# A planner that fences GpSimd's instructions behind VectorE's, and counts slack from TensorE's present lag

## The chip, the cores and the metric

The kernel runs on one core of one Trainium2 chip. Five engines with an instruction queue each work side by side: TensorE (PE; its weight loads are listed as PEld), VectorE (DVE), ScalarE (ACT), GpSimd (POOL) and SyncE (SP), which issues the transfers between HBM and on-chip memory. The metric is the time of one execution on the device in microseconds (us).

## The reference

Three layers, the output of one being the input of the next; inputs are float32.

```python
# attention: q, k, v are (4, 8, 576, 64)
scores = scale * np.matmul(q, k.transpose(0, 1, 3, 2))
mask = (rel >= 0) & (rel < 128)                       # rel = query position - key position
scores = np.where(mask, scores - slope[head] * abs(rel), -1e9)
x = softmax(scores) @ v                               # -> (2304, 512)

# mixture: w_gate (512, 8), w1 (8, 512, 1024), w2 (8, 1024, 512)
P = np.exp(x @ w_gate - max)
for _ in range(8):
    P /= P.sum(1, keepdims=True) + 1e-09
    P /= P.sum(0, keepdims=True) + 1e-09
    P *= N / E
x = sum(P[:, e:e + 1] * (np.maximum(x @ w1[e], 0.0) @ w2[e]) for e in range(8))

# last layer: w_in (512, 2048), w_out (2048, 512)
h = x @ w_in
out = np.maximum(0.01 * h, h) @ w_out
```

## The kernel before

The 2304 tokens form 18 tiles of 128, in five groups `p` of up to two tile pairs (`PAIRS`). Attention goes tile by tile: scores (L570), exponentials, transposed probabilities (L651), values (L669). The two feed-forward layers are cut into 20 chunks of 512 hidden columns, 16 of the mixture and 4 of the last layer. Each chunk is multiplied by a scheme of seven block products (`PRODUCTS`), whose operands are sums and differences of blocks; every float32 operand is a pair of float16 numbers, a high part that ScalarE rounds (L803) and a low part that GpSimd subtracts (L804). The first product of a chunk is L1089 (banks `s`, `sq`), the second L1205 (banks `t`).

Around TensorE the work is shared like this. ScalarE copies `s` to `q` (L1101, L1113) and rounds `h` (L1136, L1142, L1158). VectorE combines bank and copy (`sq`, L1105), makes the sums `s` and some low parts `h` (L1117; L1108 in attention), and adds `t` to the output `acc` (L1218). GpSimd makes the low part of the four sums (`h`, L1161, one for each half of a unit, 180 in all), adds `part` to `acc` (L1216), makes the block sums of the weights (`raw`, `t2`, L964) and their low parts (`w`). For two of seven products, ScalarE's `part` (L1215) and GpSimd's L1216 take the place of L1218. Each chunk's weights are scaled by a power of two, through a diagonal `dg` that VectorE makes (L780).

Between 234 and 1108 us of the trace, beside the mixture's chunks, the last layer's weights, which arrive as 64-bit words, are turned into float32 in 32 pieces, up to three a chunk: VectorE's L1018 takes the exponent, ScalarE's L1021 scales it, VectorE's L1024 adds the sign and L1029 takes the mantissa, ScalarE's L1030 and L1036 convert, GpSimd's L1038 and L1042 put the number together, SP stores it.

The order on every engine is made by a planner (`Plan`) while the kernel is built. All instructions are recorded first. `weigh` gives each a cost; VectorE's instructions that read and write on-chip memory alone, without a PSUM bank, are marked `shared`, since they use a port to that memory together with GpSimd. `deadlines` works back from TensorE's products, laid end to end, to the latest time at which each instruction may end (`latest`). `order` then plays the program through: at each step it takes the engine that can start first, among its ready instructions the one with the earliest `latest`, and tries some swaps. `fix` nails the result down as a fixed order on every engine. Between engines, an instruction waits only for the data and the buffers that it needs.

Of the kernel before, what the change touches and what calls it, by code (L numbers as in the profile page):

```python
# [30 lines left out]
class Plan:  # L31
# [13 lines left out]
    LANDING = 2000.0  # L45
    PER_NS = 350.0
    NEAR = 60.0

    def __init__(self, nc, tc, slots, before, after):
        self.tc = tc  # L50
# [192 lines left out]
    def deadlines(self, products):  # L243


        nodes = self.nodes
        n = len(nodes)
        ends, t, mode = {}, 0.0, "full"
        for i in products:
            t += nodes[i]["cost"] + self.TURN.get((mode, nodes[i]["mode"]), 0)  # L250
            mode = nodes[i]["mode"]
            ends[i] = t
        latest = [ends.get(i, t + 5000) for i in range(n)]
        left = [len(self.behind[i]) + len(self.softly[i]) for i in range(n)]
        room = dict.fromkeys(self.START, t + 5000)
        heap = [(-latest[i], -i) for i in range(n) if not left[i]]
        heapq.heapify(heap)
        while heap:
            i = -heapq.heappop(heap)[1]
            a = nodes[i]  # L260
            eng = a["eng"]
            if eng not in ("PE", "SP"):
                latest[i] = min(latest[i], room[eng])
                room[eng] = latest[i] - a["cost"] + self.START[eng]
            for k in a["before"] | a["starts"] | a["soft"]:
                b = nodes[k]
                end = latest[i] - a["cost"] + (b["cost"] if k in a["starts"] else -self.latency(b, a))
                latest[k] = min(latest[k], end)
                left[k] -= (k in a["before"]) or (k in a["starts"])
                left[k] -= k in a["soft"]  # L270
                if not left[k]:
                    heapq.heappush(heap, (-latest[k], -k))
        return latest

    def order(self, latest):
        nodes, behind = self.nodes, self.behind
        n = len(nodes)
        left = [len(node["before"]) + len(node["starts"]) for node in nodes]
        ready, free = [0.0] * n, dict.fromkeys(self.START, 0.0)
# [5 lines left out]
        empty = {tag: [0.0] * bufs for tag, bufs in self.room.items()}  # L285
        using = {name: len(u) for name, u in self.users.items()}
        closed = dict.fromkeys(self.users, 0.0)
        gpsimd, port, mode = (0.0, 0.0), (0.0, 0.0), "full"
        self.starts = [0.0] * n

        def since(i):

# [9 lines left out]
        def takes(i, t):  # L302

            node = nodes[i]
            cost = node["cost"]
            if node["eng"] == "PE":
                cost += self.TURN.get((mode, node["mode"]), 0)
            elif node["shared"] and gpsimd[0] <= t < gpsimd[1]:
                cost = max(cost, gpsimd[1] - t + cost - node["shared"])
            elif node["eng"] == "Pool" and port[0] <= t < port[1]:  # L310
                cost += max(0.0, port[1] - t - 140)
            return cost

        for _ in range(n):
            choices = []
            for e, w in waiting.items():
                when = [(x, i) for x, i in ((since(i), i) for i in w) if x is not None]
                if when:
                    choices.append((max(free[e], min(when)[0]), e, when))
            t, eng, when = min(choices)  # L320
            at = dict((i, x) for x, i in when)
            near = t + (self.NEAR if eng != "PE" else 0)
            pick = min((i for i in at if at[i] <= near), key=lambda i: (latest[i], i))
            start = max(t, at[pick])
            cost = takes(pick, start)
            if eng != "PE" and eng != "SP":

                for i in sorted((i for i in at if i != pick and at[i] < start + cost), key=lambda i: latest[i]):
                    s = max(at[i], t)
                    c = takes(i, s)  # L330
                    if (latest[i] < latest[pick] and max(at[i], start + cost) + nodes[i]["cost"] > latest[i]
                            and s + c + nodes[pick]["cost"] <= latest[pick]):
                        pick, start, cost = i, s, c
                        break
                if nodes[pick]["shared"] and cost > nodes[pick]["cost"] + 100:
                    other = [i for i in at if i != pick and not nodes[i]["shared"] and at[i] <= start + 100
                             and max(t, at[i]) + nodes[i]["cost"] + cost <= max(latest[pick], start + cost + 200)]
                    if other:
                        pick = min(other, key=lambda i: latest[i])
                        start = max(t, at[pick])  # L340
                        cost = takes(pick, start)
            node = nodes[pick]
            end = start + cost
            if eng == "PE":
                mode = node["mode"]
            elif node["shared"]:
                port = (max(start, gpsimd[1]) if gpsimd[0] <= start < gpsimd[1] else start), end
            elif eng == "Pool":
                gpsimd = start, end
            self.starts[pick] = start  # L350
            free[eng] = end - (self.START[eng] if cost > 100 else 0)
            waiting[eng].remove(pick)
            for tag, _ in node["opens"]:
                empty[tag].remove(min(empty[tag]))
            for name in node["uses"]:
                using[name] -= 1
                closed[name] = max(closed[name], end + (self.FROM_PE if eng == "PE" else 60))
                if not using[name] and name in self.tag_of:
                    empty[self.tag_of[name]].append(closed[name])
            orders[eng].append(pick)  # L360
            for k in behind[pick]:
                ready[k] = max(ready[k], start if pick in nodes[k]["starts"] else end + self.latency(node, nodes[k]))
                left[k] -= 1
                if not left[k]:
                    waiting[nodes[k]["eng"]].append(k)
        self.length = end
        return orders

    def fix(self):
        follows = mybir.DependencyInfo(mybir.DependencyClass.NoSync, mybir.DependencyReason.DATA)  # L370
        products = [i for i, node in enumerate(self.nodes) if node["eng"] == "PE"]
        for picks in self.order(self.deadlines(products)).values():
            line = [ins for i in picks for ins in self.nodes[i]["ins"]]
            for a, b in zip(line, line[1:]):
                self.tc.add_manual_dep(b, a.name, follows, reason="order")


@with_exitstack
# [1115 lines left out]
```

## Time and profile before

| | |
|---|---|
| median of 3 runs | 1856.25 us (1854.02 to 1857.41) |
| the profiled execution | 1853.38 us, span of its records 1851.6 us |
| granted TensorE clock in it | 0.996 of full speed |
| busy: TensorE, its weight loads | 1812.1 us (98%), 1603.7 us (87%) |
| busy: VectorE, ScalarE, GpSimd | 1367.5 (74%), 1348.8 (73%), 1323.0 us (71%) |
| transfers | 97.8 MB, 53 GB/s in the mean |

Busy time is the union of an engine's instructions. An instruction's time includes time in which it has been taken up and is held by a port, so a VectorE or GpSimd instruction that takes longer than its equals was held up. Matmuls are pipelined and their ends modelled: the idle time noted before a matmul is what is lost.

### The profile page before, as it was taken

What the parts mean: (1) busy time and instruction counts of PE and PEld (TensorE: products, weight loads), DVE (VectorE), ACT (ScalarE), POOL (GpSimd) and SP (SyncE); (2) the same over time, 40 slices, a digit from 0 to 9 for tenths busy, and PEclk for the clock granted to TensorE, in tenths of its full rate; (3) what the DMA queues carried; (4) which work ended last, traced back from release to release, by engine and by line L of the source; (5) the groups of instructions that cost most, each with busy time, mean ns of one, the idle gap of its engine ahead of it and who ended that gap; (6) DMA issues with size and microseconds to landing.
All of it is one profiled execution on the core that took longest, in us unless ns stands there. A gap on an engine that the chain in (4) does not pass through costs nothing.

```text
span 1851.6 us, 45040 instructions
## 1 busy us (share of the span) xinstructions
PE 1812.1 (98%) x17542; PEld 1603.7 (87%) x17542; DVE 1367.5 (74%) x3656; ACT 1348.8 (73%) x3099; POOL 1323.0 (71%) x1154
## 2 busy tenths in 40 slices
PE   8899999999999999999999999999999999999999
PEld 6677888889888888889888888889898888989888
DVE  7878677777777687777777776666676888687877
ACT  8988778767767766767767667666666789877664
POOL 3943878787869788787868777676667696776753
PEclk9999999999999999999999999999999999999999
DMA  8332020311112121202111110100000000101002
GB/s 296 109 115 76 4 81 28 87 37 62 53 47 67 32 74 37 86 27 72 53 47 53 47 52 30 47 24 24 24 24 34 15 24 24 47 1 47 1 33 72
DMA packets 61096, 97.81 MB, mean 53 GB/s; under 512 B 4561, under 2 KB 27601, under 8 KB 60881
## 3 DMA queue, kind: packets, MB, share of 16 engines
q1 hardware_dynamic: 60880, 94.93, 15.6%
q8 instruction: 137, 2.24, 0.5%
q14 instruction: 79, 0.64, 0.1%
HBM read 81.81 MB, written 13.11 MB: 51 GB/s over the span
## 4 chain that ended last, share of the span: by engine, by line
PE 76%; POOL 7%; ACT 6%; DVE 5%; DMA 4%; issue 2%; SPq 0%; POOLq 0%; DVEq 0%; ACTq 0%
PE t L1205 36%; PE s L1089 20%; PE sq L1089 15%; POOL w L804 3%; DMA raw<-in_moe_w_dram 3%; POOL h L1161 1%; PE s L570 1%; PE o L669 1%; PE pt L651 1%; ACT junk L937 1%; POOL xp L804 1%; DVE s L1117 1%; DVE raw L1018 1%; ACT raw L940 1%; DVE acc L1218 1%
## 5 line engine op out<-in xcount | busy, mean ns | idle before, releaser
L1205 PE MATMUL t<-w,h 128*128 128x256 f16 x7560 | 953.3, 273 | 7.5 <-ACT acc L1212 2.7
L1089 PEld LDWEIGHTS <-w 128*128 128x128 f16 x8400 | 757.0, 98 | 101.5 <-issue 22.9
L1205 PEld LDWEIGHTS <-h 128*128 128x128 f16 x7560 | 736.1, 98 | 97.1 <-issue 8.8
L1089 PE MATMUL s<-xp,w 128*128 128x256 f16 (+1 forms) x4872 | 591.3, 262 | 13.4 <-ACT q L1101 10.2
L1218 DVE SCALAR_TENSOR_TENSOR acc<-t,pu,acc 128x256 f32<-128x256 f32 x866 | 407.3, 479 | 173.5 <-PE t L1205 149.9
L1161 POOL TENSOR_TENSOR h<-s,h 128x1024 f16<-128x1024 f32 x180 | 386.2, 2145 | 135.1 <-ACT h L1158 95.4
L1089 PE MATMUL sq<-xp,w 128*128 128x256 f16 (+1 forms) x3528 | 429.9, 262 | 1.8 <-ACT q L1101 1.0
L1216 POOL TENSOR_TENSOR acc<-acc,part 128x256 f32<-128x256 f32 x322 | 238.9, 743 | 201.0 <-ACT part L1215 131.5
L804 POOL TENSOR_TENSOR w<-raw,w 128x512 f16<-128x512 f32 x240 | 274.7, 1162 | 28.8 <-ACT w L803 28.3
L1101 ACT ACTIVATE q<-s 128x256 f32<-128x256 f32 x364 | 138.6, 381 | 134.9 <-PE s L1089 132.3
L1158 ACT ACTIVATE h<-s 128x1024 f16<-128x1024 f32 x180 | 190.1, 1056 | 45.8 <-DVE s L1117 44.4
L1117 DVE SCALAR_TENSOR_TENSOR h<-sq,h 128x512 f16<-128x512 f32 x352 | 193.1, 553 | 34.0 <-ACT h L1136 24.4
L1215 ACT ACTIVATE part<-t,pu 128x256 f32<-128x256 f32 x322 | 152.1, 472 | 79.8 <-PE t L1205 75.0
L1105 DVE SCALAR_TENSOR_TENSOR sq<-s,q 128x256 f32<-128x256 f32 x176 | 75.8, 431 | 143.5 <-PE s L1089 86.3
L1105 DVE SCALAR_TENSOR_TENSOR sq<-sq,q 128x256 f32<-128x256 f32 x352 | 150.3, 427 | 38.1 <-PE sq L1089 33.6
L803 ACT ACTIVATE w<-raw 128x512 f16<-128x512 f32 x240 | 147.5, 631 | 12.1 <-PE s L1089 4.3
L1117 DVE SCALAR_TENSOR_TENSOR s<-sq,s 128x256 f32<-128x256 f32 x352 | 146.4, 416 | 0.7
L1136 ACT ACTIVATE h<-sq 128x512 f16<-128x512 f32 x176 | 104.9, 596 | 55.6 <-DVE sq L1105 46.5
L1117 DVE SCALAR_TENSOR_TENSOR s<-sq,q 128x256 f32<-128x256 f32 x352 | 137.1, 417 | 9.4 <-ACT q L1113 7.8
L940 ACT ACTIVATE raw<-raw,sr 128x512 f32<-128x512 f32 x160 | 109.7, 720 | 7.4 <-DVE sr L795 7.4
L937 ACT ACTIVATE junk<-raw 128x512 bf16<-128x512 f32 x160 | 100.4, 627 | 14.6 <-DMA raw<-in_moe_w_dram 9.1
L964 POOL TENSOR_TENSOR raw<-raw 128x512 f32<-128x512 f32 x80 | 102.4, 1280 | 0.0
(151 smaller groups left out, 1682.9 us busy)
## 6 DMA issues: line engine op xcount, KB each, us to landing
raw<-in_moe_w_dram SPq DMA_DIRECT2D x32, 768.0 KB, 4.7
k_t<-in_k_dram SPq DMA_DIRECT2D x16, 512.0 KB, 4.6
raw<-in_moe_w_dram SPq DMA_DIRECT2D x32, 256.0 KB, 3.6
raw<-in_moe_w_in_dram SPq DMA_DIRECT2D x16, 512.0 KB, 3.5
raw<-in_moe_w_out_dram SPq DMA_DIRECT2D x16, 512.0 KB, 3.5
q_t<-in_q_dram SPq DMA_DIRECT2D x18, 256.0 KB, 2.9
acc<-in_v_dram SPq DMA_DIRECT2D x18, 256.0 KB, 6.1
v_t<-in_v_dram SPq DMA_DIRECT2D x18, 256.0 KB, 2.7
```

Of the source, the lines that this page charges most:

```text
L803: nc.scalar.activation(out=hi, in_=src, func=AF.Copy)
L804: return nc.gpsimd.tensor_tensor(out=lo, in0=src, in1=hi, op=ALU.subtract)
L1089: nc.tensor.matmul(d[b][:, f, :], t[:, wp, kk, ft * P:(ft + 1) * P], XP[p][:, o, kk, xp, :], start=(i == 0 and f == 0 and j in FIRST), sto ...
L1101: nc.scalar.activation(out=q[:, k], in_=ps, func=AF.Copy, scale=CS)
L1105: nc.vector.scalar_tensor_tensor(out=block(k), in0=ps, scalar=CS, in1=q[:, k], op0=ALU.mult, op1=ALU.add)
L1117: nc.vector.scalar_tensor_tensor(out=out, in0=in0, scalar=sc, in1=in1, op0=op0, op1=op)
L1158: nc.scalar.activation(out=h[:, 3:7, 0, :], in_=d["s"], func=AF.Copy)
L1161: nc.gpsimd.tensor_tensor(out=h[:, 3:7, 1, :], in0=d["s"], in1=h[:, 3:7, 0, :], op=ALU.subtract)
L1205: nc.tensor.matmul(ps, h[:, o, hp, f, tt * P:(tt + 1) * P], w[:, wp, ft, :], start=(i == 0 and j in FIRST), stop=(i == 5), skip_group_chec ...
L1215: nc.scalar.activation(out=part, in_=ps, func=AF.Copy, scale=s)
L1216: nc.gpsimd.tensor_tensor(out=dst, in0=dst, in1=part, op=ALU.add)
L1218: nc.vector.scalar_tensor_tensor(out=dst, in0=ps, scalar=s, in1=dst, op0=ALU.mult, op1=ALU.add)
```

## The change

Four things change in the planner, and nothing in the kernel that it orders (whose lines stand 39 further down).

1. `order` remembers the last VectorE instruction on the port (`holder`). Where GpSimd's next instruction is planned to start later than that one and within 1500 ns of its start (`GUARD`), the pair goes into `turns`, and `fix` makes GpSimd's instruction wait for the other's end with a semaphore. In the plan GpSimd starts after it as well; before, GpSimd's cost was lengthened instead.
2. Before GpSimd is given an instruction, `claim` looks for a VectorE instruction on the port that costs over 230 ns and can start within 400 ns (`REACH`). If it makes nothing more urgent late, VectorE goes first.
3. A VectorE instruction that would start during GpSimd's may be planned for GpSimd's end instead, so that another one goes ahead of it.
4. `lag` is the most by which a planned product has ended after its ideal end. The tests of whether something is late use `latest + lag`.

```diff
+    REACH = 400.0
+    GUARD = 1500.0
...
-            elif node["eng"] == "Pool" and port[0] <= t < port[1]:
-                cost += max(0.0, port[1] - t - 140)
...
+                if e == "DVE" and gpsimd[1] > free[e]:
+                    when = [(max(x, gpsimd[1]) if nodes[i]["shared"] and gpsimd[0] <= max(x, free[e]) < gpsimd[1]
+                             and latest[i] + lag > gpsimd[1] + nodes[i]["cost"] else x, i) for x, i in when]
...
+            if eng == "Pool":
+                if holder is not None:
+                    t = max(t, port[1] + self.TO["Pool"])
+                first = min((i for _, i in when if since(i) <= t + self.NEAR), key=lambda i: (latest[i], i), default=None)
+                wanted = self.claim(choices, latest, lag, free["DVE"], t, first)
+                if wanted is not None:
+                    eng, when = "DVE", [wanted]
+                    t = max(free["DVE"], wanted[0])
...
-                    if (latest[i] < latest[pick] and max(at[i], start + cost) + nodes[i]["cost"] > latest[i]
-                            and s + c + nodes[pick]["cost"] <= latest[pick]):
+                    if (latest[i] < latest[pick] and max(at[i], start + cost) + nodes[i]["cost"] > latest[i] + lag
+                            and s + c + nodes[pick]["cost"] <= latest[pick] + lag):
...
+                lag = max(lag, end - self.ends[pick])
...
+                if holder is not None and start < port[0] + self.GUARD:
+                    self.turns.append((pick, holder))
+                holder = None
...
+    def claim(self, choices, latest, lag, free, t, first):
+
+        for _, e, when in choices:
+            if e == "DVE":
+                for x, i in sorted(when, key=lambda w: latest[w[1]]):
+                    a = self.nodes[i]
+                    start = max(free, x)
+                    if a["shared"] and a["cost"] > 230 and start <= t + self.REACH:
+                        late = start + a["cost"]
+                        if any(k != i and max(y, late) + self.nodes[k]["cost"] > latest[k] + lag and latest[k] < latest[i]
+                               and y <= late for y, k in when):
+                            return None
+                        if first is not None and latest[first] < latest[i] and late + self.nodes[first]["cost"] > latest[first] + lag:
+                            return None
+                        return x, i
+        return None
...
+        after = mybir.DependencyInfo(mybir.DependencyClass.Sync, mybir.DependencyReason.DATA)
+        for i, k in self.turns:
+            self.tc.add_manual_dep(self.nodes[i]["ins"][0], self.nodes[k]["ins"][-1].name, after, reason="port")
```

110 instructions of GpSimd get such a wait: 41 behind L780, 47 behind L1018 or L1029, 22 in attention and set-up behind other steps; 25 of the 110 are `h` (L1161). TensorE's order changes in 1213 of its 33026 rows (rows of equal instructions that follow each other), VectorE's in some 400 of 3525, ScalarE's in some 335 of 2675, GpSimd's in some 130 of 1136; a third to a half of these rows stand in the first fifth of the program.

GpSimd in the chunk that runs at 903 us of the trace, before (numbers are those of the buffers; the bracket names the engines whose semaphores the instruction waits for; L1161 makes `h`, L964 sums weights, L1216 adds to the output):

```order
L964 TENSOR_TENSOR t2_13765<-raw1_174 128x512 [waits Pool_49]
L1161 TENSOR_TENSOR h_13815<-s_13946,h_13815 128x4x256 [waits Activation_49]
L964 TENSOR_TENSOR raw1_174<-raw1_174,t2_13765 128x2x256 [waits Pool_49]
L1216 TENSOR_TENSOR acc12_110<-acc12_110,part_14026 128x256 [waits DVE_49,Activation_49]
L964 TENSOR_TENSOR raw1_174<-raw1_174 128x2x256
L1216 TENSOR_TENSOR acc14_112<-acc14_112,part_14092 128x256 [waits Activation_49]
```

and after the change:

```order
L1003 TENSOR_TENSOR t2_13765<-raw1_174 128x512 [waits Pool_49]
L1200 TENSOR_TENSOR h_13815<-s_13946,h_13815 128x4x256 [waits DVE_49,Activation_49]
L1255 TENSOR_TENSOR acc12_110<-acc12_110,part_14026 128x256 [waits DVE_49,Activation_49]
L1003 TENSOR_TENSOR raw1_174<-raw1_174,t2_13765 128x2x256 [waits Pool_49]
L1255 TENSOR_TENSOR acc14_112<-acc14_112,part_14092 128x256 [waits Activation_49]
L1003 TENSOR_TENSOR raw1_174<-raw1_174 128x2x256
```

`h_13815` waits for VectorE now, and the two L964 on `raw1` (L1003 after the change) stand behind `acc12` and `acc14`, with `acc12` ahead of the first. VectorE's order at this place is the same before and after; GpSimd's `h_13815` waits for L1057 of these rows of the change (L1018 before it) and `acc12` for L1068 (L1029):

```order
L1257 SCALAR_TENSOR_TENSOR acc12_110<-t0_13996,pu_12705,acc12_110 128x256 [waits PE_49]
L1057 TENSOR_SCALAR raw0_173<-raw0_173 128x512 [waits DMAHW1_49,Pool_49]
L1144 SCALAR_TENSOR_TENSOR sq_14004<-sq_14004,q_13987 128x256 [waits PE_49,Activation_49]
L1257 SCALAR_TENSOR_TENSOR acc11_109<-t0_13893,pu_12705,acc11_109 128x256 [waits PE_49]
L1063 SCALAR_TENSOR_TENSOR raw0_173<-raw0_173,sign_88 128x512 [waits Activation_49]
L1068 TENSOR_SCALAR raw0_173<-raw0_173 128x512 [waits DMAHW2_49]
L1144 SCALAR_TENSOR_TENSOR sq_14004<-s0_13988,q_13987 128x256 [waits DVE_49,PE_49,Activation_49]
L1144 SCALAR_TENSOR_TENSOR sq_14029<-sq_14029,q_13987 128x256 [waits PE_49]
```

The two casts were there before as well, unfenced: what moved is on GpSimd alone. Six more chunks get the same pair of waits, and four others a like one. GpSimd in attention, around 80 us, where the first chunk's `h_853` and `h_1013` are made (`pieces` are the softmax's inverses, `w1` the low parts of weights), before:

```order
L804 TENSOR_TENSOR w1_729<-t2_681,w1_729 128x512 [waits Activation_49]
L804 TENSOR_TENSOR w1_732<-raw1_174,w1_732 128x512 [waits Activation_49]
L804 TENSOR_TENSOR w1_735<-raw1_174,w1_735 128x512 [waits Activation_49]
L618 TENSOR_TENSOR pieces_164<-pieces_164 128x8 [waits DVE_49,PE_49]
L618 TENSOR_TENSOR pieces_164<-pieces_164 128x8 [waits Pool_49]
L1161 TENSOR_TENSOR h_853<-s_996,h_853 128x4x256 [waits Activation_49]
L804 TENSOR_TENSOR w1_738<-raw1_174,w1_738 128x512 [waits Activation_49]
L804 TENSOR_TENSOR w1_741<-raw1_174,w1_741 128x512 [waits Activation_49]
L1161 TENSOR_TENSOR h_1013<-s_1161,h_1013 128x4x256 [waits Activation_49]
```

and after:

```order
L657 TENSOR_TENSOR pieces_164<-pieces_164 128x8 [waits DVE_49,PE_49]
L657 TENSOR_TENSOR pieces_164<-pieces_164 128x8 [waits DVE_49,Pool_49]
L843 TENSOR_TENSOR w1_729<-t2_681,w1_729 128x512 [waits DVE_49,Activation_49]
L1200 TENSOR_TENSOR h_853<-s_996,h_853 128x4x256 [waits DVE_49,Activation_49]
L1200 TENSOR_TENSOR h_1013<-s_1161,h_1013 128x4x256 [waits DVE_49,Activation_49]
L843 TENSOR_TENSOR w1_732<-raw1_174,w1_732 128x512 [waits Activation_49]
L843 TENSOR_TENSOR w1_735<-raw1_174,w1_735 128x512 [waits Activation_49]
L843 TENSOR_TENSOR w1_738<-raw1_174,w1_738 128x512 [waits Activation_49]
L843 TENSOR_TENSOR w1_741<-raw1_174,w1_741 128x512 [waits Activation_49]
```

Both `h` now follow each other and wait for VectorE's steps L1156 (L1117 before), and four weight splits stand behind them; two of those had stood between the two `h`, and two before the first.

## Rows read from the trace of the kernel before

**Rows 1.** Stretches: length; busy us (instructions) of PE, PEld, DVE, ACT, POOL; clock, DMA.

```profile
0.00:100.00 100.00, 85.42 (x817) 64.56 (x818) 77.68 (x286) 89.50 (x280) 61.38 (x78) 0.97 0.61 200
100.00:200.00 100.00, 95.45 (x1039) 75.76 (x1038) 72.72 (x255) 81.77 (x248) 49.26 (x59) 0.98 0.24 76
...
300.00:900.00 600.00, 596.69 (x5737) 535.73 (x5735) 438.65 (x1098) 432.64 (x939) 474.20 (x397) 1.00 0.17 54
900.00:1100.00 200.00, 192.18 (x1841) 171.75 (x1840) 149.35 (x353) 136.34 (x297) 153.36 (x130) 0.99 0.17 58
```

**Rows 2.** TensorE's waits from 200 us on: us in total, times, longest.

```profile
PE s L1089 <- ACT q L1101: 7.6, 6, 2.6
PE s L1089 <- DVE sq L1105: 1.7, 6, 0.7
```

**Rows 3.** Three VectorE lines: xcount, ns min/median/max, first and last start, shapes.

```profile
L1018 DVE TENSOR_SCALAR raw<-raw x32: 414/650/4328, 234.1 to 1100.7; 128x512 int32<-128x512 int32 x32
...
L1029 DVE TENSOR_SCALAR raw<-raw x32: 416/422/2346, 238.6 to 1107.7; 128x512 int32<-128x512 int32 x32
...
L780 DVE TENSOR_SCALAR dg<-identb,e x51: 203/378/1916, 16.0 to 1704.2; 128x128 bf16<-128x128 bf16 x51
```

**Rows 4.** Timeline at 903 us: start, us, engine, line, tiles, count, idle before.

```profile
902.13 1.29 POOL L964 TENSOR_TENSOR t<-raw 128x512 f32<-128x512 f32 x1
...
903.05 3.96 DVE L1018 TENSOR_SCALAR raw<-raw 128x512 int32<-128x512 int32 x1
...
903.36 2.14 POOL L1161 TENSOR_TENSOR h<-s,h 128x1024 f16<-128x1024 f32 x1
```

**Rows 5.** Timeline, the same place, further on.

```profile
905.45 1.28 POOL L964 TENSOR_TENSOR raw<-raw,t 128x512 f32<-128x512 f32 x1
...
908.09 0.82 PE L1089 MATMUL s<-xp,w 128*128 128x256 f16 x6 [2.21 <-ACT q L1101]
```

**Rows 6.** Timelines of the next two chunks, where TensorE goes on.

```profile
994.68 0.82 PE L1089 MATMUL s<-xp,w 128*128 128x256 f16 x6 [2.21 <-ACT q L1101]
...
1081.91 0.82 PE L1089 MATMUL s<-xp,w 128*128 128x256 f16 x6 [2.58 <-ACT q L1101]
```

**Rows 7.** Timeline of an earlier chunk, 485 to 491 us.

```profile
485.39 0.65 DVE L1018 TENSOR_SCALAR raw<-raw 128x512 int32<-128x512 int32 x1
...
485.70 2.32 POOL L1161 TENSOR_TENSOR h<-s,h 128x1024 f16<-128x1024 f32 x1
...
486.83 1.74 DVE L1024 SCALAR_TENSOR_TENSOR raw<-raw,sign 128x512 int32<-128x512 int32 x1
...
488.49 1.49 DVE L1029 TENSOR_SCALAR raw<-raw 128x512 int32<-128x512 int32 x1
...
490.37 0.81 PE L1089 MATMUL s<-xp,w 128*128 128x256 f16 x6 [0.19 <-DVE sq L1105]
```

**Rows 8.** GpSimd's `h` and `acc`: busy, mean ns, idle before and its releaser.

```profile
L1161 POOL TENSOR_TENSOR h<-s,h 128x1024 f16<-128x1024 f32 x180 | 386.2, 2145 | 135.1 <-ACT h L1158 95.4
...
L1216 POOL TENSOR_TENSOR acc<-acc,part 128x256 f32<-128x256 f32 x322 | 238.9, 743 | 201.0 <-ACT part L1215 131.5
```

**Rows 9.** Timelines in attention, 82 to 87 and 181 to 187 us.

```profile
82.96 4.53 DVE L1117 SCALAR_TENSOR_TENSOR h<-q,h 128x768 f16<-128x768 f32 x2
...
83.09 0.66 PE L651 MATMUL pt<-ident,e 128*128 128x128 f32 x4 [1.15 <-DVE pb L656]
...
86.73 0.61 PE L1205 MATMUL t<-w,h 128*128 128x256 f16 x2 [1.56 <-POOL h L1161]
...
181.53 1.39 DVE L855 TENSOR_TENSOR h<-acc,acc 128x256 f32<-128x256 f32 x1
...
183.98 0.81 PE L1205 MATMUL t<-w,h 128*128 128x256 f16 x6 [1.36 <-DVE k L786]
...
186.62 0.77 PE L1205 MATMUL t<-w,h 128*128 128x256 f16 x3 [1.82 <-ACT acc L1212]
```

**Rows 10.** TensorE's second product: busy, mean ns, idle before and its releasers.

```profile
L1205 PE MATMUL t<-w,h 128*128 128x256 f16 x7560 | 953.3, 273 | 7.5 <-ACT acc L1212 2.7 <-POOL h L1161 1.6 <-DVE k L786 1.4
```

More of the change, by code (lines that the diff above doesn't have):

```diff
@@ L252, in deadlines @@
             ends[i] = t
+        self.ends = ends
         latest = [ends.get(i, t + 5000) for i in range(n)]
@@ L287, in order @@
         closed = dict.fromkeys(self.users, 0.0)
-        gpsimd, port, mode = (0.0, 0.0), (0.0, 0.0), "full"
+        gpsimd, port, mode, holder = (0.0, 0.0), (0.0, 0.0), "full", None
         self.starts = [0.0] * n
+        self.turns = []
+        lag = 0.0
         def since(i):
@@ L336, in order @@
                     other = [i for i in at if i != pick and not nodes[i]["shared"] and at[i] <= start + 100
-                             and max(t, at[i]) + nodes[i]["cost"] + cost <= max(latest[pick], start + cost + 200)]
+                             and max(t, at[i]) + nodes[i]["cost"] + cost <= max(latest[pick] + lag, start + cost + 200)]
                     if other:
@@ L345, in order @@
                 mode = node["mode"]
+                lag = max(lag, end - self.ends[pick])
             elif node["shared"]:
                 port = (max(start, gpsimd[1]) if gpsimd[0] <= start < gpsimd[1] else start), end
+                holder = pick
             elif eng == "Pool":
                 gpsimd = start, end
+                if holder is not None and start < port[0] + self.GUARD:
+                    self.turns.append((pick, holder))
+                holder = None
             self.starts[pick] = start
```

## The prediction

> **What bounds the kernel now.** TensorE. I read the stretches first: TensorE is busy for 596.69 of the 600 us from 300 to 900, but only for 192.18 of the 200 us from 900 to 1100, and in the first 200 us, where attention runs, for 85.42 and 95.45 of 100 each [rows 1]. So its idle time, which is all that an order can win, lies in two places: 14.6 + 4.6 = 19.1 us in attention, and 7.8 us between 900 and 1100. VectorE (some 73% busy between 300 and 900) and GpSimd (79%) have room of their own; they matter only where TensorE waits for them.
>
> Then I asked, from 200 us on, whom TensorE waits for. The largest entry is ScalarE's `q` (L1101): 7.6 us in six waits, the longest 2.6. VectorE's `sq` (L1105) follows with 1.7 us in six [rows 2]. A wait for ScalarE need not be ScalarE's fault, so I went to the timeline there.
>
> At 903.05 VectorE starts the first cast step L1018 and is listed as busy for 3.96 us. The same instruction, with the same shape, takes 0.414 us at its shortest and 0.650 in the median [rows 3]. GpSimd is in the sum L964 when it starts, begins the 2.14 us `h` (L1161) at 903.36 and another L964 after it, all back to back; VectorE gets through only when the second L964 ends [rows 4, 5]. Behind it, in VectorE's fixed order, stand the `sq` and `acc` steps, behind ScalarE's L1021 stands its L1101, and TensorE's matmul at 908.09 has idled for 2.21 us. The same picture stands at 990 (2.21) and 1077 (2.58) [rows 6]. The sum of the three is 7.0 us: nearly all of the 7.8.
>
> Now an earlier chunk, 418 us before, with the same order. At 485.39 L1018 again arrives just before GpSimd's L964 ends, but this time it gets in, in 0.65 us, and `h`, listed from 485.70 with 2.32 us, is the one that waits [rows 7]. In both chunks the order is the same and `h` is listed 0.31 us after L1018, yet L1018's time differs by 3.3 us: who takes the port is a race that the order leaves open. In this chunk the later steps lose smaller ones: L1024 takes 1.74 us and L1029 1.49, and TensorE has idled 0.19 us at 490.37 [rows 7].
>
> **The change, part by part.**
>
> *The wait in the cast's place (A).* In the chunk at 903 VectorE's order is unchanged; `h` now waits until L1018 is done, the next GpSimd instruction `acc12` waits for L1029, and the two L964 move behind `acc12` and `acc14`. L1018 then waits only for the L964 that runs, 0.3 us, and takes its 0.41, so ScalarE's L1021 and L1101 come some 3.2 us earlier. `h` starts 0.4 to 0.5 us later. What hides that is the time in which GpSimd's `h` waits for others anyway: 135.1 us in all before its 180 runs [rows 8]. I take all of 7.0 us back. The bounds are 3.5 (half, if something else is late next) and 7.0.
>
> *The same wait in the other cast chunks (B).* There L1018 won anyway. What is new is that `acc12` waits for L1029, so L964 can't slip in between L1024 and L1029: L1029 falls from 1.49 us to its median of 0.42 [rows 3], and the `sq` that TensorE waits for comes 1 us earlier. All of such waits are 1.7 us; I take 1.2, with bounds of 0 and 1.7. L1024 isn't helped: `h` still goes ahead of it. GpSimd idles about 1 us more a chunk, in front of an accumulation that has 201.0 us of idle time before it in all [rows 8].
>
> *Attention (C).* Here much is reordered, not only fenced. Port losses show in two places. At 82.96 two VectorE `h` steps together take 4.53 us beside GpSimd's `h`; TensorE has idled 1.15 us at 83.09 and 1.56 at 86.73 [rows 9]. In the new order `h_1013` follows `h_853` directly, with two weight splits no longer between them, and both wait for VectorE's steps. Around 182 the sums L855, one at 1.39 us, and the scale steps behind them run against GpSimd's splits; TensorE has idled 1.36 us at 183.98 and 1.82 at 186.62 [rows 9]. In the new order each of those three splits waits for one L855. The four are 5.9 us. Since ScalarE's and VectorE's orders before 250 us change in hundreds of rows by a rule that no trace has tried, I take half, 3.0 us. The bounds: 5.9 won, and 6 lost (a third more than today's 19.1 idle).
>
> *The waits themselves (D).* 110 of GpSimd's instructions get one: 41 behind a scale step L780, 47 behind L1018 or L1029, the rest in attention and set-up. One costs GpSimd at most what VectorE still has to do: 0.2 to 0.4 us where VectorE runs freely [rows 3], more where VectorE's step itself waits in its queue. Queued behind the waiting instruction is all of GpSimd's work: `h`, the weight splits, the accumulations; who waits for those is TensorE. TensorE's 7560 L1205 matmuls wait for GpSimd's `h` for 1.6 us in the whole trace [rows 10]. So I price D at 1.0 us, between nothing and the last rival's 20.
>
> *Slack from the present lag.* It takes no instruction away. It lets the planner's swap tests work again late in the program, where TensorE is behind its ideal and every plain deadline is past. Its effect is part of the reordering in A to C. SP's queue of transfers changes in five places, all before 300 us: a weight load moves behind the next loads of q and k, and one cast load ahead of a store. The weights that it fetches are the second chunk's, and ScalarE's steps on them stand later in the new order too, so I give it no term.
>
> Sum: 7.0 + 1.2 + 3.0 - 1.0 = 10.2 us. The profiled execution took 1853.4 us, which gives 1843.2. That execution is 2.9 us below the runs' median of 1856.25 (1854.0 to 1857.4). A race that goes one way or the other at each cast would give just such a spread, and the new order has fewer; so I put the median less than 1 us above its sum: **1844 us**.
>
> **A rule beside the row.** At 903 a VectorE step that was already waiting when GpSimd finished was passed over, twice [rows 4, 5]. The Trainium skill's page "SBUF — State Buffer" (section "SBUF: two separate sides") says that the pair of ports shared by the two engines is an exclusive lock: whichever instruction starts first has it for its whole length, and the other fully blocks. By that rule the trace agrees that one blocks fully, but the page doesn't say who comes next. If it were the one that has waited longest, L1018 would never lose more than the rest of one GpSimd instruction, and an order that fences GpSimd would win nothing in the cast chunks: 2.0 us in all, against 10.2 by the row.
>
> **The rivals.**
> - *The port serves who waits.* L1018's 3.96 us would then have another cause, A and B vanish, and C minus D leaves 2.0 us: 1851.4, as a median 1852. [rows 4, 5] speak against it. 5%.
> - *Attention gives it back.* TensorE's order is nearly kept in attention, but ScalarE's weight work for the next chunk moves by many rows. If attention loses 6 us in place of winning 3, the sum is 7.0 + 1.2 - 6.0 - 1.0 = 1.2 us: 1852.2, as a median 1853, no change that can be told. For it speaks that 19 us of idle time there have many small causes; against it, that both big ones are port losses. 17%.
> - *More is won.* If before's other runs lose more casts than the profiled one, and all of C comes: 7.0 + 1.7 + 5.9 plus one or two smaller scale-step collisions (L780 takes 0.38 us in the median, up to 1.92 [rows 3]), some 17 us: 1837. 10%.
> - *Slower: GpSimd waits at the wrong moment.* 25 of the new waits stand on `h`. If L1018 or L780 stands in VectorE's queue behind a step that waits for TensorE, `h` waits for TensorE as well, and TensorE soon waits for `h`. At 0.8 us each that is 20 us: 1853.4 - 10.2 + 20 = 1863. From 0.4 us each on it outweighs the gain. Against it: at 903 and at 485 L1018 stood ready before GpSimd came to `h` [rows 4, 7], and TensorE hardly waits for `h` now. 10%.
> - *As summed*: 58%, with a range of its own of 1838 to 1850.
>
> **How the numbers follow.** 0.2%, 3.7 us, is about what a measurement of this kernel tells from no change. Faster than 1852.5: 58 + 10 + 7 of the 22 of the first two rivals, 0.75. Within it: 0.15. Slower: 0.10. The range runs from 1835 (A, B and C at their best bounds, 14.6 us, and a few collisions more) to 1856 (attention's loss); it leaves out the slower case and a little on either side.
>
> **What would show it.** L1018's longest falls from 4.33 us to below 1.5, and L1029's median stays with its longest below 1.2; L780's mean falls. TensorE's idle time from 900 to 1100 falls from 7.8 us to 2 or less: A right. TensorE's waits for `sq` (L1105) below 1 us: B right. TensorE busy for over 184 of the first 200 us: C right; below 178 would make it wrong, and the forecast with it. GpSimd's idle time before `h` and `acc` grows, with VectorE's busy time down by 15 us or more, and TensorE's waits for `h` stay below 3 us: D right. The forecast fails if TensorE's waits for GpSimd grow past 6 us, or if the three stalls return as waits of another name.

## The result, and the profile after

The changed kernel took 1836.75 us in the median of four runs (1834.8 to 1838.0), beside 1856.83 for the kernel before on the same chip: a ratio of the means of 0.9878, interval [0.9834, 0.9923] (one of before's four runs took 1869.0; the medians alone give 0.9892). Measured once more it took 1837.71, a ratio of 0.9894 [0.9880, 0.9908]. So it is faster by 1.1 to 1.2%, some 20 us. I had forecast 1844. Direction and places were right, but I had worked out 10.2 us; from one profiled execution to the other (1853.38 to 1834.78 us) it is 18.6.

Lines stand 39 further down now: L1018 is L1057, L1029 L1068, L1161 L1200, L780 L819, L1105 L1144, L1218 L1257. The stretches of the changed kernel, with the columns of [rows 1]:

```profile
0.00:100.00 100.00, 88.00 (x843) 66.65 (x844) 74.30 (x292) 88.55 (x275) 58.90 (x79) 0.97 0.62 203
100.00:200.00 100.00, 95.04 (x1034) 75.79 (x1033) 71.29 (x258) 86.48 (x259) 49.95 (x59) 0.98 0.24 73
300.00:900.00 600.00, 599.02 (x5770) 539.01 (x5768) 431.78 (x1110) 433.16 (x939) 470.53 (x400) 1.00 0.17 54
900.00:1100.00 200.00, 200.00 (x1956) 180.39 (x1955) 143.28 (x368) 144.41 (x316) 155.61 (x133) 1.00 0.18 62
```

TensorE has no idle time left from 900 to 1100 us (7.8 before) and 1.0 us from 300 to 900 (3.3 before). Its waits from 200 us on, as in [rows 2]:

```profile
PE xt L916 <- DVE k L828: 1.6, 1, 1.6
PE t L1244 <- DVE acc L1257: 1.3, 2, 0.9
PE sq L1128 <- DVE s L1156: 0.7, 2, 0.4
PE s L1128 <- ACT q L1140: 0.5, 2, 0.3
```

The wait for ScalarE's `q`, 7.6 us before, is down to 0.5, and a wait for `sq` isn't listed. The three VectorE lines of [rows 3] (ns at shortest, median, longest):

```profile
L1057 DVE TENSOR_SCALAR raw<-raw x32: 414/427/1303, 232.8 to 1083.4; 128x512 int32<-128x512 int32 x32
L1068 DVE TENSOR_SCALAR raw<-raw x32: 413/419/426, 236.4 to 1085.3; 128x512 int32<-128x512 int32 x32
L819 DVE TENSOR_SCALAR dg<-identb,e x51: 203/249/1232, 16.0 to 1685.6; 128x128 bf16<-128x128 bf16 x51
```

The longest cast fell from 4.33 to 1.30 us. The timeline of the chunk of [rows 4, 5], which runs at 896 us now (start, length, engine, line; in brackets the idle time before it and what ended it):

```profile
895.05 1.28 POOL L1003 TENSOR_TENSOR t<-raw 128x512 f32<-128x512 f32 x1
...
895.96 0.66 DVE L1057 TENSOR_SCALAR raw<-raw 128x512 int32<-128x512 int32 x1
...
896.77 2.13 POOL L1200 TENSOR_TENSOR h<-s,h 128x1024 f16<-128x1024 f32 x1 [0.43 <-DVE raw L1057]
...
897.41 2.03 DVE L1063 SCALAR_TENSOR_TENSOR raw<-raw,sign 128x512 int32<-128x512 int32 x1
...
899.37 0.42 DVE L1068 TENSOR_SCALAR raw<-raw 128x512 int32<-128x512 int32 x1
...
899.93 0.73 POOL L1255 TENSOR_TENSOR acc<-acc,part 128x256 f32<-128x256 f32 x1 [1.03 <-DVE raw L1068]
```

The cast gets in when the running sum ends, `h` waits 0.43 us for it, the second step is still blocked by `h` (2.03 us; it takes 0.74 alone), and GpSimd waits 1.03 us so that the third step takes its 0.42. The groups of [rows 8] on the page:

```profile
L1200 POOL TENSOR_TENSOR h<-s,h 128x1024 f16<-128x1024 f32 x180 | 383.9, 2133 | 132.1 <-ACT h L1197 76.2
L1255 POOL TENSOR_TENSOR acc<-acc,part 128x256 f32<-128x256 f32 x322 | 234.3, 729 | 194.3 <-ACT part L1254 75.7
```

GpSimd's idle time before both is lower than before (135.1 and 201.0), though I had said that it would grow. VectorE's busy time fell from 1367.5 to 1329.2 us, as I had said.

### The profile page after: what moved, and what is told of

It reads as the page before. It is cut to its first block, busy times and chain, and to the rows that moved or that the text cites. A ratio compares the mean times of both kernels' runs of the same rounds, so it can differ in the third digit from the quotient of the medians.

```text
span 1833.0 us, 45057 instructions
## 1 busy us (share of the span) xinstructions
PE 1807.0 (99%) x17542; PEld 1603.2 (87%) x17542; DVE 1329.2 (73%) x3656; ACT 1350.1 (74%) x3099; POOL 1310.8 (72%) x1154
## 4 chain that ended last, share of the span: by engine, by line
PE 71%; ACT 2%; DVE 2%; DMA 1%; POOL 1%; issue 0%; SPq 0%; ACTq 0%
PE t L1244 36%; PE s L1128 20%; PE sq L1128 15%; DMA raw<-in_moe_w_dram 1%; DVE sx L930 0%; DVE s L1156 0%; ACT acc L917 0%; POOL w L843 0%; ACT junk L976 0%; ACT h L1197 0%; PE xt L916 0%; POOL h L1200 0%; DVE acc L1257 0%; ACT raw L979 0%; ACT q L1140 0%
## 5 line engine op out<-in xcount | busy, mean ns | idle before, releaser
L1257 DVE SCALAR_TENSOR_TENSOR acc<-t,pu,acc 128x256 f32<-128x256 f32 x866 | 406.6, 479 | 179.0 <-PE t L1244 151.0
L1200 POOL TENSOR_TENSOR h<-s,h 128x1024 f16<-128x1024 f32 x180 | 383.9, 2133 | 132.1 <-ACT h L1197 76.2
L1255 POOL TENSOR_TENSOR acc<-acc,part 128x256 f32<-128x256 f32 x322 | 234.3, 729 | 194.3 <-ACT part L1254 75.7
L1156 DVE SCALAR_TENSOR_TENSOR h<-sq,h 128x512 f16<-128x512 f32 x352 | 193.0, 553 | 30.5 <-ACT h L1175 24.4
L1144 DVE SCALAR_TENSOR_TENSOR sq<-s,q 128x256 f32<-128x256 f32 x176 | 75.9, 431 | 149.1 <-PE s L1128 91.9
L1144 DVE SCALAR_TENSOR_TENSOR sq<-sq,q 128x256 f32<-128x256 f32 x352 | 150.2, 427 | 37.7 <-PE sq L1128 34.3
L1156 DVE SCALAR_TENSOR_TENSOR s<-sq,s 128x256 f32<-128x256 f32 x352 | 146.1, 415 | 0.7
L1156 DVE SCALAR_TENSOR_TENSOR s<-sq,q 128x256 f32<-128x256 f32 x352 | 136.7, 417 | 10.6 <-ACT q L1152 8.8
L1003 POOL TENSOR_TENSOR raw<-raw 128x512 f32<-128x512 f32 x80 | 102.0, 1275 | 0.4 <-DVE dg L819 0.4
```

Source lines behind the costliest of these rows:

```text
L1144: nc.vector.scalar_tensor_tensor(out=block(k), in0=ps, scalar=CS, in1=q[:, k], op0=ALU.mult, op1=ALU.add)
L1156: nc.vector.scalar_tensor_tensor(out=out, in0=in0, scalar=sc, in1=in1, op0=op0, op1=op)
L1200: nc.gpsimd.tensor_tensor(out=h[:, 3:7, 1, :], in0=d["s"], in1=h[:, 3:7, 0, :], op=ALU.subtract)
L1255: nc.gpsimd.tensor_tensor(out=dst, in0=dst, in1=part, op=ALU.add)
L1257: nc.vector.scalar_tensor_tensor(out=dst, in0=ps, scalar=s, in1=dst, op0=ALU.mult, op1=ALU.add)
```

## The experiments

All of them in one table. The ratio is to the kernel before on the same chip, whose medians were 1856.0 to 1857.7. The last two columns are from the trace of one execution and split it at a fixed place: when the 201st of the 7560 matmuls of L1205 starts (some 36 us behind the start of the last L669 matmul, which I call the last attention value), and the time from there to TensorE's last instruction. The same number of matmuls lies ahead of that place in every run but the three without lag or claim, which have 6 to 12 fewer there, so that some 1 us of their work stands under "rest". "No claim" leaves out the holding back of VectorE as well; the two were not tried apart.

```
                                          median   ratio [interval]         201st   rest
before                                    1856.25                           215.6  1632.7
before, another execution                 1856.8                            217.4  1634.4
changed                                   1836.75  0.9878 [0.9834, 0.9923]  212.1  1617.6
changed, again                            1837.7   0.9894 [0.9880, 0.9908]  211.4  1621.1
on the order of before:
  lag alone                               1858.8   1.0011 [0.9996, 1.0025]  217.9  1642.7
  waits, first cast step only             1854.0   0.9985 [0.9966, 1.0003]  217.5  1632.7
  waits, all cast steps                   1844.5   0.9944 [0.9929, 0.9960]  220.4  1624.8
  the same, another execution             1845.0                            217.3  1622.6
  all waits                               1846.6   0.9946 [0.9928, 0.9964]  221.4  1624.4
on new orders, all waits, planner counts them:
  no claim, no lag                        1842.7   0.9920 [0.9907, 0.9933]  212.6  1622.7
  claim, no lag                           1839.8   0.9916 [0.9902, 0.9929]  211.8  1621.4
  lag, no claim                           1837.4   0.9902 [0.9887, 0.9917]  211.5  1620.4
  both, reach 200                         1835.9   0.9885 [0.9871, 0.9898]  211.5  1619.4
  both, reach 1000                        1838.1   0.9911 [0.9896, 0.9926]  210.9  1621.7
the changed kernel's orders:
  no waits                                1858.8   1.0009 [0.9995, 1.0023]  214.6  1639.8
  waits behind casts only                 1845.3   0.9931 [0.9917, 0.9946]  216.0  1626.2
  the other waits only                    1853.4   0.9974 [0.9957, 0.9991]  214.1  1636.9
```

**Is who gets the port a race?** The kernel before, unchanged, in another execution.

> The kernel before, profiled once more, to see whether the same casts lose the port. If it is a race by small differences of time, other casts than those at 903, 990 and 1077 us lose in this execution, or another number of them, and the times of the two executions differ by about 3.3 us for each. If the order fixes it, the same three lose and TensorE idles for 7 to 8 us between 900 and 1100 again.

Other casts lost: those at 572, 827 and 1079 us. The first of them, with GpSimd around it and the matmul that idled:

```profile
572.24 3.70 DVE L1018 TENSOR_SCALAR raw<-raw 128x512 int32<-128x512 int32 x1 [0.16 <-DMA raw<-in_moe_w_in_dram]
572.32 2.12 POOL L1161 TENSOR_TENSOR h<-s,h 128x1024 f16<-128x1024 f32 x1
...
574.40 1.25 POOL L964 TENSOR_TENSOR raw<-raw,t 128x512 f32<-128x512 f32 x1
...
577.02 0.82 PE L1089 MATMUL s<-xp,w 128*128 128x256 f16 x6 [2.19 <-ACT q L1101]
```

In the first execution the cast of this chunk won. One order, two outcomes: a race. The Trainium skill's page "SBUF — State Buffer" (section "SBUF: two separate sides") has the pair of ports as an exclusive lock for whoever starts first. Both executions agree that the other fully blocks, 3.70 us for 0.42 of work. Which of two that wait comes next that section doesn't say; here the cast, listed 0.08 us ahead of `h`, came behind it, and the two executions show that the order doesn't settle it.

**Waits or orders?** The changed kernel's orders without the semaphores (below); the lines of `holder`, `turns` and `fix` in the planner of before, whose order they leave as it was; the lines of `lag` alone in it.

```diff
-        for i, k in self.turns:
+        for i, k in self.turns[:0]:
```

> The changed kernel's orders on every engine, with the 110 waits left out. Theory F (the waits decide who takes the port): without them the casts L1057 lose the port to h and L1003 again in several chunks, the longest over 3 us, and the time returns most of the way, to 1845 to 1855 us. Theory O (the new order has put the port's users apart, the waits only confirm it): the longest L1057 stays below 2.1 us and the time stays within 3 us of the changed kernel, 1834 to 1840. If TensorE's clock falls again after a stall near 900 to 1100 us, the loss per lost cast should be nearer 3.3 us (10.0 over three) than 2.3 (7.0 over three).

> The planner and the orders of before, with the waits alone added behind the same kind of VectorE step (no claim, no holding back of VectorE, no lag). Theory F: the three lost casts of 903, 990 and 1077 us are gone, TensorE's idle time from 900 to 1100 falls from 7.8 to below 2 us, and the time falls by 8 to 15 us, to 1841 to 1849; attention keeps most of its 19 us of idle time. Theory O: nothing or a loss, 1852 to 1865, because GpSimd comes to its waits at the wrong time.

> The planner of before, with slack counted from TensorE's present lag in its two swap tests and nothing else. Theory F: no gain that can be told, 1853 to 1860, casts still lost at some places. Theory L (the lag makes the late part of the program better planned, and that is where the gain beyond my sum came from): 1840 to 1849, with TensorE's idle time from 900 us on down by 8 us or more.

The orders alone won nothing (1858.8 us, more than the 1855 that theory F had as its most) and the lag alone nothing; in the lag's profiled execution five casts took 3.9 to 4.3 us, and at 1866 us it was the longest of its runs. The waits alone won 0.54%, half of the whole. Theory F held for the waits, with one correction: without them, no cast of the new orders took over 3 us in the profiled execution (the longest took 2.73), and still it lost as much, in other waits. TensorE's waits there:

```profile
PE t L1244 <- DVE acc L1257: 4.8, 10, 0.9
PE sq L1128 <- ACT q L1140: 4.5, 3, 2.5
PE s L1128 <- ACT q L1140: 3.1, 6, 1.0
```

**Which waits on the old order?** Only those behind the three cast steps (61 of that order's 126: 20 behind the first step, 13 behind the second, 28 behind the third), then only those behind the first step.

```diff
-                if holder is not None and start < port[0] + 1500.0:
+                if holder is not None and start < port[0] + 1500.0 and any("int32" in r[5] for r in nodes[holder]["reads"]):
```

The casts alone read whole numbers; the first step is told from the others by its one operand and the place that it writes.

> The order of before, with waits only where GpSimd comes behind a cast step (an instruction that reads whole numbers: lines L1018, L1024, L1029 of the kernel before); the other waits of the run with waits alone are left out. It prices terms A and B without attention. My sum had 7.0 + 1.2 = 8.2 us for them. The three lost casts of the second execution of before (572, 827 and 1079 us) show 2.4 us of start-to-start loss each, and a fall of TensorE's clock behind one of them; by that, 8 to 11 us, 1846 to 1849 us. If the waits in attention and behind the scale steps did the work, 1853 to 1857.

> The order of before with waits behind the cast steps, one more look. Its first profiled execution was the longest of six (1850.3 us, the others 1843.0 to 1846.2) and had its last attention value at 184.4 us, 4.9 later than the kernel before. If that belongs to the execution, the value comes at 179 to 182 us here and the time is 1843 to 1847; if the waits do it, at 184 again, and 1848 or more.

> The order of before, with waits only behind the first cast step (L1018 of the kernel before): 20 of the 61 waits of the run with cast waits. If my term B is right (the waits behind the last cast step win 1.2 us), this run is 1 us or more slower than that with all cast waits (1844.5), and L1029 takes up to 2.3 us again. If those waits cost as much as they win, since the sums acc12 behind them come later, it is as fast, 1842 to 1846 us, and TensorE waits less than 3.7 us for VectorE's acc.

The waits behind all cast steps give all that waits give on this order, and somewhat more than I had expected (1844.5 us, beside 1846 to 1849; the third of the casts that I worked it out from lost 2.7 us, not 2.4). The late end of attention in the first execution (184.4 us) was its own: the other has 181.3 us, like the second execution of before (181.4). With waits behind the first step alone, no cast L1026 (L1018 before) takes over 2.21 us, so the three big stalls are gone, and yet almost nothing is won. The chunk of 903 in that kernel, and TensorE's largest wait:

```profile
911.63 2.13 POOL L1169 TENSOR_TENSOR h<-s,h 128x1024 f16<-128x1024 f32 x1 [0.42 <-DVE raw L1026]
...
913.72 1.71 POOL L972 TENSOR_TENSOR raw<-raw,t 128x512 f32<-128x512 f32 x1
914.23 1.49 DVE L1037 TENSOR_SCALAR raw<-raw 128x512 int32<-128x512 int32 x1
...
916.11 0.81 PE L1097 MATMUL s<-xp,w 128*128 128x256 f16 x6 [0.48 <-DVE sq L1113]
```

```profile
PE s L1097 <- DVE sq L1113: 5.8, 11, 1.0
```

The first step goes first, and GpSimd's sum L972 then meets the third step (L1037, L1029 before) in place of the first: 1.49 us, and the `sq` behind it is late, in 11 places, 5.8 us. It is the waits behind the later steps that turn the first one's into a gain. By these rows that is the third step's; the second's were left out together with it, but among the changed kernel's 47 waits behind casts none stands behind the second. The later waits have a price on the old order, where `acc` comes later: with all cast waits TensorE waits for VectorE's `acc` 3.7 and 2.9 us in the two executions; with the first step's alone 1.3.

```profile
PE t L1213 <- DVE acc L1226: 3.7, 8, 1.0
```

**What makes the other half?** The changed kernel without lag, without claim and holding back, and without all three.

```diff
-                lag = max(lag, end - self.ends[pick])
```
```diff
-                if e == "DVE" and gpsimd[1] > free[e]:
+                if False:
...
-                wanted = self.claim(choices, latest, lag, free["DVE"], t, first)
+                wanted = None
```

> The changed kernel with slack counted as before (the lag held at 0); waits, claim and the holding back of VectorE stay. The waits alone on the order of before gave 1846.6 us, the lag alone 1858.8, the new order without waits 1858.8, all together 1836.8; so some 10 us come from an order that was made for the waits. Theory G (the claim and the holding back of VectorE make that order): 1836 to 1841 us here. Theory L (once the waits make the planner's times true, the lag's swaps pay): 1845 to 1850 us, as with the waits alone.

> The changed kernel without the claim and without the holding back of VectorE; waits and lag stay. Theory G: 1845 to 1850 us, about what the waits alone gave on the order of before. Theory L: 1836 to 1841 us. If both this and the kernel without lag come out at 1846, the two pay only together.

> The changed kernel without the claim, without the holding back of VectorE and without the lag: what stays is the waits and a planner that starts GpSimd's next instruction only when VectorE's is over. Waits on the order of before gave 1846.6 and 1844.5 us, waits with claim 1839.8, waits with lag 1837.4, waits with both 1836.8. Theory M (what pays beside the waits is that the planner's times count them): 1836 to 1841 us here too, and the last attention value comes at about 176 us, as in those three. Theory S (claim or lag is needed, either of the two): 1844 to 1848 us, last attention value at 180 us or later.

> The changed kernel once more, on the same chip and at the same time as its parts. No theory says other than 1834 to 1839 us. By all of them no cast L1057 takes over 1.5 us, the last attention value comes at 176 us within 1.5, and the times spread by less than the 10.2 us that 23 runs of before did in the first call (1852.5 to 1862.8), since a race of 2.4 to 4.0 us for each lost cast is gone.

Neither theory alone: without the lag the time is where theory G had put it (1839.8), without the claim where theory L had (1837.4), and without both it lies between those of M and S (1842.7). A planner that merely counts the waits takes 0.26% off what the waits give on the old order. In the traces it all lies ahead of the split: the 201st L1205 matmul comes at 212.6 us (217.3 to 221.4 with waits on the old order), and the rest takes as long (1622.7; 1622.6 to 1624.8). How much of that is the planner's isn't shown: ahead of the split this execution, the fastest of its five, has a mean granted clock of 0.99 (3.4 us at the half level), the three on the old order 0.95 to 0.97 (13.6 to 23.8 us), while TensorE's idle time differs by 2.2 to 3.3 us only.

Lag and claim take 1 to 5 us off the rest: 1620.4 and 1621.4 by one of them, 1617.6, 1621.1 and 1619.4 by both (1621.7 at a reach of 1000). These are single executions, and the changed kernel's own two are 3.5 us apart. Together the two are shown by the times: measured side by side on one chip, the runs without them took 1840.5 to 1843.6 us and those of the changed kernel 1835.3 to 1839.3. Apart they are not shown: by the ratios the lag is worth 0.18% (3.3 us), but the two intervals overlap; the claim alone is worth 0.04, and the claim on top of the lag 0.08, which can't be told from nothing. With both, at a reach of 200 or 400 ns, TensorE's wait for `acc` is 1.2 to 1.3 us (3.2 with neither), and the scale steps L780 are short, 16.9 to 18.1 us in sum for 51 (28.8 with neither, 29.0 before).

**The claim's reach**, `REACH` 200 and 1000 in place of 400.

> The changed kernel with a claim that looks 200 ns ahead in place of 400. If the claim's size matters, it lies between the run without claim (1837.4) and the changed kernel (1836.8), or beside a best value; if only waits and planner matter, 1835 to 1840 us whatever the reach, as at 1000 ns (1838.1).

> The changed kernel with a claim that looks 1000 ns ahead in place of 400, so that GpSimd lets more VectorE steps go first. In the changed kernel L1063 (L1024 before) is still blocked for 1.29 us by h at 11 places and no wait of TensorE hangs on it. If blocked VectorE steps still cost, 1829 to 1835 us; if they have become free and GpSimd's lateness counts now, 1837 to 1850.

Neither can be told from the changed kernel's 0.9894 [0.9880, 0.9908]; 200 ns has the lowest median of all, 1835.9. At 1000 ns the second cast step is freed (25.1 us in sum, longest 1.6, where the changed kernel has 34.1 and 2.04), and the time doesn't move: nothing on TensorE's path hung on it.

**Which waits on the new orders?** The 47 behind casts, or (with a `not` ahead of `any`) the other 63.

```diff
-                if holder is not None and start < port[0] + self.GUARD:
+                if holder is not None and start < port[0] + self.GUARD and any("int32" in r[5] for r in nodes[holder]["reads"]):
```

> The changed kernel's orders, with only the 47 of the 110 waits that stand behind a cast step (they read whole numbers); those behind L780's scale step, in attention and in the set-up are left out. The new orders without any wait gave 1858.8 us. If the orders win attention by themselves (last attention value at 176 us), only the casts need waits and the time is 1836 to 1841 us. If attention needs its waits, the last attention value comes at 179 to 181 us and the time is 1840 to 1848.

> The changed kernel's orders with the 63 waits that are not behind a cast step: those behind L780's scale step, in attention and in the set-up. No wait gave 1858.8 us, cast waits alone 1845.3, all of them 1837 to 1838. If the two kinds add up, 1849 to 1852 us here, with the last attention value at 176 us (180 without them). If attention's gain came from the orders or from something else, 1855 to 1859 and 180 us.

With the runs with none and with all they make a square: +0.09% with none, -0.69 with casts only, -0.26 with the others only, -1.06 with all. The two kinds add up (0.78 + 0.35 = 1.13 from the run with none, beside 1.15). The time with the others only, 1853.4, lies between my two cases. The last attention value comes at 180.2 us with none, 180.0 with casts only, 178.2 with the others only, and 176.2 and 175.7 with all (on the old order 179.6 to 184.4 in five executions without waits there, 184.1 with all waits): attention's gain needs its new order and its waits, and neither alone gives it. The casts start at 232 us only, so 178.2, 176.2 and 175.7 have the same instructions and waits ahead of them: a single execution tells this value to some 2 us.

## Why the prediction fell short

**Bound and cause: right.** The three stalls were a lost race for the port, and the second execution of before shows it as a race. The rival that the port serves who waits is out.

**C, attention: right in its place, and somewhat small.** 3.0 us forecast; the 201st L1205 matmul comes 3.5 us earlier (4.2 and 4.1 in the executions of the changed kernel again and with reach 200). Before's 215.6 us is also the earliest of the five executions that have its attention (215.6 to 220.4, mean 217.6); by that mean the gain is 5.5 to 6.2 us. TensorE was busy 183.0 of the first 200 us, short of the 184 I had named.

**A and B: the sum was about right, the split wrong.** 8.2 us, less D's 1.0, against 7.9 and 10.1 in the two traces with cast waits on the old order (1632.7 to 1624.8 and 1622.6). But I put 7.0 down to the cast's getting in, and gave the wait behind the last step 1.2 in the other chunks, counting each stall at today's place, although A names that wait in the lost chunks too. Alone the waits behind the first step won 0.0 us of 1632.7 in their execution (0.15% by runs, not clear of noise); those behind the later steps made the rest. I had seen the collision of L964 with L1029 in the chunk at 485, where the cast had won [rows 7], and did not ask whether the lost chunks would become like it. They did.

A's stalls were also dearer than their idle marks (2.21, 2.21, 2.58 [rows 5, 6]): from start to start of the matmuls 2.37, 2.38 and 2.74, and behind the second the granted clock fell, for another 1.7 us (below). So "its idle time, which is all that an order can win" is wrong: of the 18.6 us between the two profiled executions TensorE's idle time gives 13.5, and the other 5.1 were listed as busy (1812.1 us before, 1807.0 after).

**D, the waits: priced at 1.0, found at nothing in the changed kernel.** From 200 us on TensorE doesn't wait for `h` there; GpSimd's idle time before `h` and `acc` even fell. On the old order the price is real, 1.6 to 2.4 us more waiting for `acc` with all cast waits than with the first step's. The new planner works round it.

**The step that failed** is "Its effect is part of the reordering in A to C": slack from the lag, and the claim with it, got no term, since I priced only what the old order's trace showed as stalls. From the 201st L1205 matmul to TensorE's end the three traces with both, at reach 200 and 400, take 1617.6 to 1621.1 us, mean 1619.4; the two with cast waits on the old order mean 1623.7: 4.3 us. The times agree: 0.26%, 4.8 us, between the kernels without both and with both. With the mean of attention's three, 3.9, and the casts' 9.0, the parts are 17.2, 7.0 above my sum. Of that 4.3 is the missing term, 1.8 the casts and D, 0.9 attention; from traces of one execution each, so the split holds to some 2 us. The number of my rival "More is won" came out, 1837, but not by its sum: that was luck.

**The start of the sum.** The profiled execution of before, 1853.4 us, was among the quicker ones: later medians are 1856.0 to 1857.7 and single runs went from 1850.6 to 1869.0. From 1853.4 to the changed kernel's median it is 16.6 us, from before's median 20. That lost casts make this spread fits the lag's 1866 us with five of them; that the changed kernel's runs spread less can't be said from four. The clock has a part as well: the granted clock of before's runs is 0.995 to 0.996 in the mean, that of the changed kernel's 0.997 and 0.998. A stretch of 3.4 us at the half level takes 0.0009 off such a mean and cost 1.4 to 1.7 us where it could be measured (below), so by my estimate 2 to 6 of the 20 us lie there; whether the stalls caused all of that isn't shown.

## What to carry to other kernels

When a fence cures the biggest stall of a chain, ask what its victim meets next: a fence on the first step of three moved the loss to the third, and it paid only together with fences on the later steps. A gain from ordering shared ports belongs to waits and planner together: orders without waits won nothing, waits without a planner that counts them half, and an estimate made from today's stalls alone misses the part that the planner wins. If one profile shows a race lost three times, take a second profile of the same kernel before pricing it by place.

## What the runs showed of the hardware

In these traces TensorE's clock fell behind some stalls of 2.4 to 2.7 us (from start to start of the matmuls) and not behind others. Of the 11 casts over 3 us in the traces of before (two executions) and of the lag alone, five had a stretch of 3.4 us at the half level (1.2 GHz) that began between 0.3 us ahead of the matmul that had idled and 1.2 us behind it; six with stalls as long had none. (The changed orders without cast waits have one such stall each, at 411 and 409 us, and a stretch behind it.) Without the fall the loss from start to start of the matmuls was 2.36 to 2.75 us in the 14 us behind the cast, with it 4.03 to 4.32, so that 1.4 to 1.7 us come on top. The stretch at 578 us in the second execution of before (the clock is the third number from the right):

```profile
578.00:581.60 3.60, 3.60 (x20) 2.61 (x18) 1.85 (x4) 2.12 (x6) 2.36 (x3) 0.53 0.02 5
```

TensorE is listed as fully busy there, with 20 matmuls in 3.6 us where it does 34 in 3.4 us at the full clock (from 832.5 us, behind a stall without a fall): idle time leaves this loss out. What decides whether the clock falls stays open, and so does what decides the race for the port: in this trace the cast's start is listed 0.08 us before `h`'s, in a won one 0.31 [rows 7], and no offset parts the won from the lost ones.
